# A gated-recurrence and expert kernel on one core: a new written-out order, first exponentials by halves of the heads, and two more turns by DMA

## The chip, the cores and the metric

One core of one Trainium2 chip. The metric is device microseconds of one execution. The kernel before has run three times: 178.1, 178.4 and 218.8 us, median 178.4. A further execution was profiled; it took 177.89 us, of which the profile covers a span of 176.1 us.

## The reference

Two stages follow each other. A gated linear recurrence over 768 steps, for 4 batches of 8 heads of width 48, and then a two-layer expert with a SiLU between:

```python
f = 1.0 / (1.0 + np.exp(-f_logit))
for t in range(S):                      # S = 768
    state = f[:, :, t, :, None] * state + np.einsum('bhd,bhe->bhde', k[:, :, t], v[:, :, t])
    y[:, :, t] = np.einsum('bhd,bhde->bhe', q[:, :, t], state)
...
x = y.transpose(0, 2, 1, 3).reshape(3072, 384)
h = x @ w_in                            # 384 x 2048
out = (h * sigmoid(h)) @ w_out          # 2048 x 384
```

## The kernel before, in words

**Tiling.** The 768 steps are cut into 6 chunks of 128, so there are 24 *units* (chunk, batch). Two units make a *pair* P, units 2P and 2P+1. In the first three pairs (units 0 to 5) the two units are two neighbouring chunks of one batch, loaded as one *block* whose rows on a partition are two steps; from unit 6 on they are the same chunk of two batches.

**One unit** is a chain of small tasks. Their names are used all through this text; `_u` is the unit, `_P` the pair.

- `f`, `k`, `q`, `v`: loads, issued on SP (L257). `E`, `L`: exponential and logarithm of the gate on ACT (L264, L266 for blocks, L268 for the rest); they give the logarithms `lf`.
- `csh_P` (a block, L335 to L339) and `cs_u` (L372, L376): running sums of `lf` over the chunk, a product with a triangle on PE. `ia`, `a` and `al` (L379, L381, L384) are exponentials of these sums, with either sign, on ACT.
- `ki`, `qg` (L386, L390): k and q times these factors, on DVE or POOL, into a buffer `qk`. Both have then to be turned (heads' width to the partitions). This is done on PE, `tq` (8 transposes, L395), with copies `qc`, `kc` or `qkc` out of PSUM (L396 to L405), or by a DMA transpose from SP, `qkD` (L407). Units 0 to 7 go by PE, units 8 to 23 by DMA.
- `sc2_P` (L280): the scores of both units of a pair, 16 matmuls. `at` (L416): their mask, two per unit, on DVE. `vb`: v in bf16.
- `y_u` (L422 with the state from before, L426): the unit's output. `d_u` (L448; in blocks from a copy of k that `dT` and `kn` turn back), `sd`, `su` (L453 to L461): the next state.
- y has to be turned as well: copied out of PSUM by `yc`, then turned on PE by `yT` (3 transposes, L434) and copied by `xc`, or by a DMA transpose, `yD` (L442). Units 0 to 13 and 22, 23 go by PE, 14 to 21 by DMA.
- `mi` (L323, 256 columns, both units of a pair at once) and `mi1` (L313, one unit, 128 columns, in the first three pairs): x times w_in, in 8 groups of a pair or 4 of a unit. `si`, `si1` (L320, L310): SiLU on ACT. `mo` (L351): times w_out, four quarters of 4 matmuls; `moh` (L357) the same by halves for the last pair. `oc`, `och`: copies out of PSUM; `so`, `soh`: stores.
- `wi`, `wo`: loads of the weights in pieces; `wic`, `woc`: their casts to bf16, in three parts each, spread over ACT, DVE and POOL. The four groups `mi1_u_0` to `mi1_u_3` need pieces 0 and 1, piece 2, piece 3 and piece 4 of w_in.
- `idle_i_n_w`: n matmuls with zeros of w columns (L291), which fill PE's waits in the first 15 us. They compute nothing.

**The order** is written out by hand: the string `PLAN` (L32 to L104) lists every task as `name/engine/slots`, and each engine runs its own tasks in that order; the slots say which numbered buffer (of 8 PSUM banks, 5 `qk` buffers, and so on, L28) a task takes. An engine does not run ahead of a task that waits. ACT needs another function table for SiLU than for exponentials and logarithms, and a table load stands wherever the order goes from one to the other (L467 to L473, issued at L499).

## Time and profile before

| what | value |
|---|---|
| profiled execution, and its span | 177.89 us, 176.1 us |
| PE (matmuls) busy | 169.5 us, 96% |
| PEld (weight loads) busy | 133.6 us, 76% |
| ACT busy | 133.3 us, 76% |
| DVE busy | 97.7 us, 55% |
| POOL busy | 59.1 us, 34% |
| ACT table loads after the first | 17, 21.8 us together |
| DMA transposes | 16 of q and k, 8 of y |
| first matmul, first one that is not fill | 1.19 us, 5.98 us |

Busy time of PE is that of overlapping matmuls: one of 384 columns is shown with 326 ns, yet twelve in a row take 1.95 us. So the step from one matmul to the next, as the chain of waits gives it for runs of equal ones, says what PE's work costs. Times in the text are microseconds from the start of the span.

### The profile page before, as it was taken

To read this page: it belongs to the slowest core of one execution; us is meant where nothing else is said; L and a number is where in the kernel's file an instruction comes from. 1 tells how busy PE (TensorE), PEld (TensorE's weight loads), DVE (VectorE), ACT (ScalarE), POOL (GpSimd) and SP (SyncE) were. 2 spreads that over 40 slices of the span, in tenths; PEclk is the share of its full clock that TensorE was granted. 3 is DMA by queue.
4 is the path that set the end of the run, shared out by engine and by line. 5 is a ranking of instruction groups with operands and counts; after the bars stand their busy time and mean duration, and the time that the engine had idled before them with its cause. 6 is when DMAs were issued, how large, how long until landed. Compare 5 with 4: busy or idle time off the path is not lost.

```text
span 176.1 us, 4798 instructions
## 1 busy us (share of the span) xinstructions
PE 169.5 (96%) x1952; PEld 133.6 (76%) x1952; DVE 97.7 (55%) x201; ACT 133.3 (76%) x249; POOL 59.1 (34%) x91
## 2 busy tenths in 40 slices
...
GB/s 147 325 286 259 397 387 220 397 207 169 217 199 241 182 238 221 159 233 232 152 197 165 251 227 89 273 176 210 137 153 99 206 162 138 217 147 0 92 90 89
DMA packets 115541, 35.17 MB, mean 200 GB/s; under 512 B 110752, under 2 KB 113056, under 8 KB 115520
## 3 DMA queue, kind: packets, MB, share of 16 engines
...
q8 instruction: 15, 0.25, 0.5%
...
HBM read 25.17 MB, written 4.72 MB: 170 GB/s over the span
## 4 chain that ended last, share of the span: by engine, by line
PE 73%; SPq 8%; DMA 8%; DVE 5%; issue 2%; POOL 2%; ACT 0%; POOLq 0%; DVEq 0%
PE ps L351 27%; PE ps L323 22%; PE ps L313 8%; SPq L257 6%; DMA wh<-in_moe_w_in_dram 5%; PE ps L280 3%; PE ps L357 3%; DMA qkT<-qk 3%; PE ps L426 2%; SPq L442 2%; DVE st L242 2%; PE ps L422 2%; PE ps L372 1%; DVE at L416 1%; PE ps L448 1%
## 5 line engine op out<-in xcount | busy, mean ns | idle before, releaser
L351 PE MATMUL ps<-w_out,hT 128*128 128x384 bf16 x352 | 66.4, 326 | 0.0
L323 PE MATMUL ps<-xT,w_in 128*128 128x256 bf16 x432 | 52.4, 273 | 0.0
L323 PEld LDWEIGHTS <-w_in 128*128 128x128 bf16 x432 | 45.3, 110 | 3.9 <-DMA xT<-yb 0.3
L320 ACT ACTIVATE hT<-ps 128x512 bf16<-128x512 f32 x72 | 39.0, 603 | 10.3 <-PE ps L323 9.6
L351 PEld LDWEIGHTS <-hT 128*128 128x128 bf16 x352 | 31.7, 97 | 16.6 <-ACT hT L310 0.3
L416 DVE TENSOR_TENSOR at<-ps,triu 128x512 bf16<-128x512 f32 x36 | 22.5, 683 | 19.8 <-PE ps L280 18.8
L242 POOL TENSOR_TENSOR qk<-q,av 128x384 bf16<-128x384 f32 x15 | 15.4, 1033 | 42.2 <-DMA q<-in_q_dram 25.0
L499 ACT ACT_TABLE_LOAD x17 | 21.8, 1283 | 0.3
L313 PE MATMUL ps<-xT,w_in 128*128 128x128 bf16 x288 | 17.9, 219 | 0.9 <-POOL w_in L239 0.6
L313 PEld LDWEIGHTS <-w_in 128*128 128x128 bf16 x288 | 16.6, 110 | 1.3 <-POOL w_in L239 0.8
L242 POOL TENSOR_TENSOR qk<-k,ia 128x384 bf16<-128x384 f32 x12 | 12.7, 1066 | 13.4 <-DMA k<-in_k_dram 8.7
L381 ACT ACTIVATE av<-ps 128x384 f32<-128x384 f32 x24 | 11.9, 504 | 3.5 <-PE ps L376 1.8
L237 DVE CAST yb<-ps 128x384 bf16<-128x384 f32 x16 | 8.8, 555 | 10.2 <-PE ps L426 9.0
L264 ACT ACTIVATE f<-f 128x768 f32<-128x768 f32 (+1 forms) x13 | 10.3, 796 | 5.4 <-DMA f<-in_f_logit_dram 5.3
L310 ACT ACTIVATE hT<-ps 128x512 bf16<-128x512 f32 x24 | 13.2, 607 | 1.6 <-PE ps L313 1.5
L453 DVE TENSOR_TENSOR sd<-ps,st 128x384 f32<-128x384 f32 x16 | 8.8, 553 | 9.5 <-ACT hT L320 4.7
L369 POOL DMA_DIRECT2D out_dram<-ob x14 | 8.0, 573 | 17.9 <-DVE ob L237 14.3
L242 POOL TENSOR_TENSOR st<-sd,al 48x192 bf16<-48x192 f32 x18 | 9.8, 543 | 8.7 <-PE ps L422 5.1
L379 ACT ACTIVATE ia<-ps 128x384 f32<-128x384 f32 x24 | 11.8, 505 | 0.0
L237 DVE COPY ob<-ps 128x384 f32<-128x384 f32 x14 | 7.7, 553 | 7.4 <-PE ps L351 3.6
L239 POOL CAST vb<-v 128x384 bf16<-128x384 f32 x11 | 5.6, 507 | 14.6 <-DMA v<-in_v_dram 13.2
L242 DVE TENSOR_TENSOR qk<-k,ia 128x384 bf16<-128x384 f32 x12 | 7.1, 605 | 5.1 <-ACT ia L379 4.2
...
## 6 DMA issues: line engine op xcount, KB each, us to landing
...
```

The source lines that it names most:

```text
L237: nc.vector.tensor_copy(o, i)
L242: (nc.vector if eng == "DVE" else nc.gpsimd).tensor_mul(*a)
L257: nc.sync.dma_start(out=dst, in_=src)
L310: return nc.scalar.activation(at("hT", u // 2)[:, 4 * m:4 * m + 4, i * C:(i + 1) * C], h, AF.Silu)
L313: nc.tensor.matmul(h[:, n, :], w_in_tile(4 * m + n, kk), at("xT", u // 2)[:, kk, i * C:(i + 1) * C], start=(kk == 0), stop=(kk == KT - 1))
L320: return nc.scalar.activation(at("hT", P)[:, 2 * j:2 * j + 2, :], h, AF.Silu)
L323: nc.tensor.matmul(h[:, i, :], w_in_tile(2 * j + i, kk), at("xT", P)[:, kk, :], start=(kk == 0), stop=(kk == KT - 1))
L351: nc.tensor.matmul(o, at("hT", P)[:, n, i * C:(i + 1) * C], w_out_sb[n // 4][:, n % 4, :], start=(n == 0), stop=(n == NT - 1))
L379: nc.scalar.activation(at("ia", u).rearrange("p h d -> p (h d)"), at("cs", u)[:, 0:HD], AF.Exp)
L381: nc.scalar.activation(at("av", u).rearrange("p h d -> p (h d)"), at("cs", u)[:, 0:HD], AF.Exp, scale=-1.0)
L416: nc.vector.tensor_mul(at("at", u)[:, r], at(f"s{r}", u).rearrange("p (n c) -> p n c", c=C), (triup if two else triu)[:, None, :].to_broad ...
L499: nc.scalar.preload_act_table_set(turn[n])
```

## The change

1. **Units turned by DMA.** q and k of unit 7 (`tq_7`, `qkc_7` become `qkD_7`) and y of unit 13 (`yT_13`, `xc_13` become `yD_13`).
2. **Halves of the heads.** In the three blocks each exponential and each logarithm is two instructions of four heads (`Eh`, `Lh`) instead of one of eight; 12 ACT instructions instead of 6. Loads stay whole.
3. **A new order.** Every line of `PLAN` differs: the order within each engine, the slots, and for many tasks the engine. Of `yc` 14 are on ACT (8 before), of `qg` 15 on DVE (9 before), 19 table loads follow the first on ACT (17 before). The fill is 29 matmuls of 512 columns and 6 of 256 (22 and 4 before). The first weights are now pieces 3 and 4 of w_in, then 1, 0 and 2, then w_out; before they were 2, 1, 0 of w_in, two pieces of w_out, and then 4 and 3.
4. `HALF = 3` becomes the set `BLOCKS = {0, 1, 2}` with the same meaning. Other new branches (weights by POOL, scores of one unit, loads of half the heads) are used by no task of the new order.

```diff
-HALF = 3
+BLOCKS = {0, 1, 2}
...
 PLAN = """
-f_0_1/SP/0 f_2_3/SP/1 k_0_1/SP/0 q_0_1/SP/0 E_0_1/ACT L_0_1/ACT/0 E_2_3/ACT idle_0_11_512/PE/0 csh_0/PE/0,1 f_4_5/SP/2 q_2_3/SP/1 v_0/SP/0 k_2_3/SP/1
...
+f_0_1/SP/0 f_2_3/SP/1 k_0_1/SP/0 q_0_1/SP/0 Eh_0_0/ACT Eh_0_1/ACT v_2/SP/0 Lh_0_0/ACT/0 Lh_0_1/ACT Eh_2_0/ACT idle_0_11_512/PE/0 csh_0/PE/0,1
...
+    def half_logs(kind, u, hf):
+        P, hs = u // 2, slice(4 * hf, 4 * hf + 4)
+        if kind == "Eh":
+            e = at("f", P).rearrange("p a h d -> p (a h d)").rearrange("p (h w) -> p h w", h=H)[:, hs]
+            nc.scalar.activation(e, e, AF.Exp, scale=-1.0)
+        else:
+            nc.scalar.activation(at("lf", P)[:, :, hs, 0:D], pairs("f", P)[:, :, hs], AF.Ln, bias=1.0)
...
+        if kind in ("Eh", "Lh"):
+            return half_logs(kind, *a)
...
-    TABLE = {**dict.fromkeys(("E", "L", "ia", "a", "al"), "natural_log_exp_and_others"), "si": "silu_and_others", "si1": "silu_and_others"}
+    TABLE = {**dict.fromkeys(("E", "L", "Eh", "Lh", "ia", "a", "al"), "natural_log_exp_and_others"), "si": "silu_and_others", "si1": "silu_and_others"}
```

The order at the start. These are DVE's rows of the kernel before, from the copies of turned q and k of the first block to the copy `xT` that the first `mi1` needs (at_115 and at_116 are the masked scores of units 0 and 1, sd a state's increment, ps a PSUM bank, yb and xT the unit's output before and after it is turned):

```order
L237 COPY qkT_112<-ps_68 128x512
L237 COPY qkT_112<-ps_67 128x8x64
L416 TENSOR_TENSOR at_115<-ps_64,triup 128x512
L416 TENSOR_TENSOR at_115<-ps_66,triup 128x512
L455 COPY sd_122<-ps_63 128x384
L416 TENSOR_TENSOR at_116<-ps_61,triup 128x512
L416 TENSOR_TENSOR at_116<-ps_68,triup 128x512
L237 COPY qkT_113<-ps_62 128x8x64
L237 COPY qkT_113<-ps_61 128x512
L237 COPY qkT_113<-ps_63 128x8x64
L237 CAST yb_120<-ps_68 128x384
L237 COPY xT_139<-ps_62 128x3x2x64
```

And DVE's rows of the change, up to its first `xT`, that of unit 1 (at_116 is unit 0 here, at_117 unit 2; st is a state, kn the keys turned back):

```order
L436 TENSOR_TENSOR at_116<-ps_66,triup 128x512
L238 COPY qkT_113<-ps_63 128x8x64
L475 COPY sd_122<-ps_68 128x384
L436 TENSOR_TENSOR at_116<-ps_65,triup 128x512
L436 TENSOR_TENSOR at_117<-ps_62,triup 128x512
L436 TENSOR_TENSOR at_117<-ps_67,triup 128x512
L243 TENSOR_TENSOR st_146<-sd_122,al_124 48x4x48 x2
L473 TENSOR_TENSOR sd_123<-ps_66,st_146 128x384
L238 COPY kn_133<-ps_62 128x512
L238 CAST yb_120<-ps_65 128x384
L243 TENSOR_TENSOR st_146<-sd_123,al_124 48x4x48 x2
L238 COPY xT_139<-ps_65 128x3x2x64
```

The masks of unit 2 and the state update of unit 0 now stand ahead of the output `yb` of unit 1, and the update of unit 1 ahead of `xT`. Before, the masks of unit 2 came behind both, the update of unit 0 was on POOL, and that of unit 1 came later.

ACT's first rows, before (f_69, f_70 are the gates of the first two blocks, lf_92 and lf_93 their logarithms; ia and av are the factors made from the running sums):

```order
L264 ACTIVATE f_69<-f_69 128x768
L266 ACTIVATE lf_92<-f_69 128x16x48
L264 ACTIVATE f_70<-f_70 128x768
L266 ACTIVATE lf_93<-f_70 128x16x48
L379 ACTIVATE ia_95<-ps_61 128x384
L379 ACTIVATE ia_96<-ps_62 128x384
L381 ACTIVATE av_98<-ps_61 128x384
```

and in the change:

```order
L276 ACTIVATE f_69<-f_69 128x384 x2
L278 ACTIVATE lf_92<-f_69 128x2x4x48 x2
L276 ACTIVATE f_70<-f_70 128x384
L278 ACTIVATE lf_93<-f_70 128x2x4x48
L276 ACTIVATE f_70<-f_70 128x384
L401 ACTIVATE av_98<-ps_62 128x384
L399 ACTIVATE ia_95<-ps_62 128x384
L401 ACTIVATE av_99<-ps_61 128x384
L278 ACTIVATE lf_93<-f_70 128x2x4x48
L404 ACTIVATE al_124<-ps_61 128x8
L399 ACTIVATE ia_96<-ps_61 128x384
```

The last half of the second block's logarithms, which `csh_1` needs, now stands behind three factors of the first block.

Later, ACT's rows around the factors of units 14 and 15, before (the rows from the logarithms of pair 8 to the next table load; ia_97 and ia_96 are of units 14 and 16; the factors of unit 15 stand a long way ahead of them):

```order
L264 ACTIVATE f_72<-f_72 128x768
L268 ACTIVATE lf_94<-f_72 128x16x48
L235 COPY xT_140<-ps_63 128x3x128
L235 COPY ob_135<-ps_62 128x384
L379 ACTIVATE ia_97<-ps_66 128x384
L381 ACTIVATE av_98<-ps_65 128x384
L384 ACTIVATE al_127<-ps_65 128x4
L381 ACTIVATE av_99<-ps_66 128x384
L379 ACTIVATE ia_96<-ps_65 128x384
L499 ACT_TABLE_LOAD
```

and in the change (av_99 and ia_97 first are unit 15, ia_96 and av_99 in the last rows unit 14, av_100 unit 17):

```order
L401 ACTIVATE av_99<-ps_65 128x384
L399 ACTIVATE ia_97<-ps_65 128x384
L404 ACTIVATE al_127<-ps_68 128x4
L404 ACTIVATE al_128<-ps_67 128x4
L399 ACTIVATE ia_96<-ps_68 128x384
L404 ACTIVATE al_124<-ps_65 128x4
L404 ACTIVATE al_129<-ps_63 128x4
L401 ACTIVATE av_100<-ps_67 128x384
L401 ACTIVATE av_99<-ps_68 128x384
L519 ACT_TABLE_LOAD
```

Between `cs_14`, from which the factors of unit 14 are made, and `sc2_7`, which needs its turned q and k, PE has in the change only `d_13`, `yT_12`, two quarters `mo` and seven groups `mi`; before, it had 36 tasks there.

More of the change, by code (lines that the diff above doesn't have):

```diff
@@ L32 @@
 PLAN = """
-f_0_1/SP/0 f_2_3/SP/1 k_0_1/SP/0 q_0_1/SP/0 E_0_1/ACT L_0_1/ACT/0 E_2_3/ACT idle_0_11_512/PE/0 csh_0/PE/0,1 f_4_5/SP/2 q_2_3/SP/1 v_0/SP/0 k_2_3/SP/1
-v_2/SP/1 v_1/SP L_2_3/ACT/1 ia_0/ACT/0 ia_1/ACT/1 a_0/ACT/0 idle_1_3_512/PE/2 csh_1/PE/2,3 al_2/ACT/0 a_1/ACT/1 a_2/ACT/2 ki_0/DVE/0 ki_1/DVE/1
-qg_2/POOL/2 qg_0/DVE qg_1/DVE idle_2_4_512/PE/4 tq_0/PE/4,5 tq_1/PE/6,7 kc_0/DVE/0 ia_3/ACT/2 E_4_5/ACT a_3/ACT/0 al_0/ACT/1 qc_0/ACT kc_1/DVE
-qc_1/DVE L_4_5/ACT/2 ia_2/ACT/0 vb_0/POOL/0 wi_2/SP/0 idle_3_4_512/PE/1 dT_0/PE/1 sc2_0/PE/5,3,0,7 csh_2/PE/4,6 qg_3/POOL/3 ki_3/POOL ki_2/POOL
@@ L37 @@
-kn_0/ACT/0 d_0/PE/2 wi_1/SP/0 wi_0/SP/1 at_0_1/DVE/0 at_0_0/DVE sd_0/DVE/0 at_1_0/DVE/1 su_0/POOL/0 idle_4_2_256/PE/1 y_0/PE/3 tq_3/PE/1,5
-idle_5_2_256/PE/2 tq_2/PE/2,0 wo_0/SP/1 a_4/ACT/1 ia_5/ACT/1 al_4/ACT/2 kc_3/ACT/1 at_1_1/DVE qc_3/DVE vb_1/ACT/1 a_5/ACT/2 yc_0/ACT/0 ia_4/ACT/2
-kc_2/DVE qc_2/DVE y_1/PE/7 dT_2/PE/5 yT_0/PE/1 sc2_1/PE/6,0,3,2 wo_1/SP/2 wic_2_2/POOL wic_2_0/POOL yc_1/DVE/1 wic_2_1/ACT vb_2/ACT/2 xc_0/DVE/0
-at_2_0/DVE/2 at_2_1/DVE dT_1/PE/4 yT_1/PE/7 dT_3/PE/1 mi1_0_1/PE/6 wi_4/SP/3 y_2/PE/0 xc_1/ACT wic_1_0/ACT wic_0_0/ACT kn_1/DVE/1 kn_2/DVE/0
```

161 lines of the change are left out of this document (89 added, 72 removed).

## The prediction

> **What bounds the kernel now.** I read the page's first part, then the stretches of time, then the chain of waits and the timelines of PE, ACT and DVE for the first 22 us.
>
> ```profile
> span 176.1 us, 4798 instructions
> PE 169.5 (96%) x1952; PEld 133.6 (76%) x1952; DVE 97.7 (55%) x201; ACT 133.3 (76%) x249; POOL 59.1 (34%) x91
> ```
>
> ```profile
> 20.00:50.00 30.00, 29.47 (x420) 24.03 (x418) 20.43 (x42) 24.78 (x49) 12.10 (x17) 1.00 1.00 276
> 50.00:170.00 120.00, 119.88 (x1311) 96.34 (x1309) 63.73 (x118) 92.11 (x167) 38.67 (x55) 1.00 0.87 176
> ```
>
> The columns of the second fence are the stretch, its length, then PE, PEld, DVE, ACT and POOL busy, the granted clock, the DMA share. From 50 to 170 us PE idles 0.12 us and its clock is full: no other order can gain there. PE is the bound; the others wait for it.
>
> What PE's work costs is read from equal runs in the chain of waits (start, length, line, count):
>
> ```profile
> 28.31 2.68 PE ps L313 x48
> 148.33 3.93 PE ps L323 x36
> 152.26 1.95 PE ps L351 x12
> 35.14 0.45 PE ps L395 x8
> 154.21 0.55 PE ps L280 x16
> 158.30 0.20 PE ps L426 x8
> 158.13 0.17 PE ps L422 x4
> ```
>
> So a group `mi1` (12 matmuls) takes 0.67, a group `mi` (6) 0.655, a quarter `mo` (4) 0.65, `tq` (8 transposes) 0.45, `dT` and `yT` with 4 and 3 of them 0.23 and 0.17, `sc2` 0.55, `y` 0.20, or 0.37 with a state, and `d`, four matmuls of the form of L422, 0.17. With them I ask of any start on PE how much work lay ahead of it; the rest of the time is lost, to waits and fill. The start shows it:
>
> ```profile
> 1.19 4.57 PE L291 MATMUL ps<-zero 128*128 128x512 bf16 x11 [1.19 <-DVE zero L477]
> 5.98 0.32 PE L335 MATMUL ps<-lf,tri 128*128 128x384 bf16 x1 [0.22 <-ACT lf L266]
> 6.83 0.81 PE L291 MATMUL ps<-zero 128*128 128x512 bf16 x3
> 7.58 0.32 PE L335 MATMUL ps<-lf,tri 128*128 128x384 bf16 x1
> 11.89 0.62 PE L280 MATMUL ps<-qkT 48*128 48x128 bf16 x16
> 18.96 0.86 PE L313 MATMUL ps<-xT,w_in 128*128 128x128 bf16 x12 [0.59 <-POOL w_in L239]
> 21.34 0.84 PE L313 MATMUL ps<-xT,w_in 128*128 128x128 bf16 x12 [0.30 <-ACT w_in L235]
> ```
>
> `csh` takes 0.85 (5.98 to 6.83). At 21.34 us PE has done three `csh` (2.55), four `tq` (1.8), four `dT` (0.9), two `sc2` (1.1), `d_0` and `d_2` (0.34), `y_0`, `y_1`, `y_2` (0.77), three `yT` (0.5), two `mi1` (1.34): 9.3. So 12.0 us are lost by then, which is nearly all that the span holds beside work and end: idle after 20 us is 0.53 and 0.12. Only the start can hold more than 1% of the time.
>
> **The change part by part.**
>
> *Turns by DMA.* `tq_7` (0.45) and `yT_13` (0.17) leave PE: −0.6, on the engine that bounds. DVE or ACT loses two copies, off the path. In their place come a transpose of q, k and one of y:
>
> ```profile
> qkT<-qk SPq DMA_TRANSPOSE x16, 4.4
> xT<-yb SPq DMA_TRANSPOSE x8, 2.3
> L407 SPq DMA_TRANSPOSE qkT<-qk x16: 1231/1269/3565, 57.0 to 148.7; - x16
> DMA to landing us min/median/max: 3.2/4.4/5.7
> ```
>
> (The last two rows belong to the tile qkT.) Each blocks SP's queue for 1.27 us at the median, and lands 4.4 or 2.3 after its issue. `qkD_7` has from the factors of unit 7 to `sc2_3` 8.7 us of PE work, `yD_13` from `y_13` to `mi_6_3` 5.5: both fit, so nothing is added on the path. Cover gone, each costs at most its latency, 4.4 and 2.3.
>
> *Halves of the heads.* A half is of the form that the loads of single units already have:
>
> ```profile
> L264 ACT ACTIVATE f<-f 128x384 f32<-128x384 f32 x2 | 1.1, 525 | 0.0
> ```
>
> and ACT's first rows in time:
>
> ```profile
> 4.21 0.84 ACT L264 ACTIVATE f<-f 128x768 f32<-128x768 f32 x1 [2.19 <-DMA f<-in_f_logit_dram]
> 5.08 0.84 ACT L266 ACTIVATE lf<-f 128x768 bf16<-128x768 f32 x1
> 5.83 0.83 ACT L264 ACTIVATE f<-f 128x768 f32<-128x768 f32 x1
> 7.44 0.85 ACT L379 ACTIVATE ia<-ps 128x384 f32<-128x384 f32 x2
> 8.18 0.49 ACT L381 ACTIVATE av<-ps 128x384 f32<-128x384 f32 x1
> 14.61 0.73 ACT L235 COPY qkT<-ps 128x512 bf16<-128x512 bf16 x1 [0.18 <-PE ps L395]
> 15.20 0.51 ACT L235 CAST vb<-v 128x384 bf16<-128x384 f32 x1
> ```
>
> A whole exponential and the logarithm that waits for it start 0.87 apart. Of halves, four start about 0.44 apart (an estimate: 525 ns less the overlap of about 0.09 that the whole ones show, 0.84 long and 0.75 apart) and need not wait for each other; the last ends near 6.05 against 5.92. So the halves alone cost 0.1 us on the first sum. Off the path the rest is hidden by PE's fill.
>
> *The order of the start.* The gate of the first block lands as before. I walk ACT from 6.05: three halves of block 1 (to 7.5), then `a_1`, `ia_1`, `a_0` at 0.37 each (7.44 to 8.18 is two), and only then the fourth half, to 9.05. So `csh_1` starts at 9.1; before, it started at 7.58. `a_2` follows at 10.05, `ia_3`, `ia_2` (its buffer comes free with `ki_1`, the fourth product on DVE since 8.7, two of which take 1.03: 11.1), `a_3`, then copies at 0.59 (14.61 to 15.20), an exponential between them: `qc_1` ends at 14.0, and `sc2_0`, which needs it, starts there and not at 11.89. Then DVE, with steps from these rows:
>
> ```profile
> 7.95 1.03 DVE L242 TENSOR_TENSOR qk<-k,ia 128x384 bf16<-128x384 f32 x2 [3.92 <-ACT ia L379]
> 13.75 0.56 DVE L455 COPY sd<-ps 128x384 f32<-128x384 f32 x1
> 14.22 1.28 DVE L416 TENSOR_TENSOR at<-ps,triup 128x512 bf16<-128x512 f32 x2
> 15.42 1.36 DVE L237 COPY qkT<-ps 128x512 bf16<-128x512 bf16 x3
> 18.82 0.74 DVE L237 COPY kn<-ps 128x512 bf16<-128x512 bf16 x2
> 17.16 0.57 DVE L237 COPY xT<-ps 128x384 bf16<-128x384 bf16 x1
> L242 DVE TENSOR_TENSOR st<-sd,al 48x192 bf16<-48x192 f32 x22 | 9.7, 440 | 0.3
> ```
>
> A mask costs 0.60 (two from 14.22 to 15.42), `sd` 0.47 (13.75 to 14.22) and `yc`, which moves as much, the same, `kn` or `qc` 0.34, `xc` 0.57, and a state update 0.75 (two of 0.44, overlapped a little like the rest). From 14.7 DVE has, in the change's order without a pause, six masks (3.6), `qc_2` (0.34), `sd_0`, `sd_1`, `yc_1` (1.4), `kn_3` (0.34), `su_0`, `su_1` (1.5) and `xc_1` (0.6): 7.8, to 22.5. `y_1` waits there for `su_0` (19.6), `yT_1` for `yc_1` (21.0), the first `mi1` stands behind `yT_1`, and the second, `mi1_1_3`, needs `xc_1`: it starts at 22.55. Ahead of it lies what lay ahead of 21.34, with `d_1` for `d_2` and one `mi1` less: 8.6. Lost: 13.9, against 12.0. That is **+1.9 us**.
>
> The weights bound this from below:
>
> ```profile
> 17.64 0.62 ACT L235 CAST w_in<-ws 128x512 bf16<-128x512 f32 x1 [0.78 <-DMA ws<-in_moe_w_in_dram]
> ```
>
> The first piece stands, as now, behind ten loads of the same size, so it lands at 17.6; three casts and a `yc` on ACT end at 20.2. Were DVE's chain no hindrance, the first `mi1` could start then, with 7.9 ahead: 12.3 lost, +0.3. From above: fourteen DVE steps with a tenth of a us of waiting each, an estimate from the 0.10 to 0.25 that lie between steps handed over in the rows, +3.3. I take the walk, since each of its steps has a row.
>
> *From there to 47 us.* Before, `mi1_4_0` starts at 47.00:
>
> ```profile
> 47.00 0.22 PE L313 MATMUL ps<-xT,w_in 128*128 128x128 bf16 x1
> ```
>
> Between 21.34 and 47.00 lie 14 `mi1` (9.4), 16 `mo` (10.4) and 5.0 of small tasks: 24.8 of 25.7, so 0.9 are lost. In the change the late weights have had two us more when PE asks, and all sums stand far ahead of their use: I take **−0.7**; bounds −0.9, and +0.3 if a cast comes late.
>
> *After 47 us.* PE's idle was 0.12; it can only grow. In the change the way from a unit's sum to its scores is short: behind `cs_14` PE has `yT_12`, `d_13`, two `mo` and seven `mi`, 6.2 us, until `sc2_7`; behind `cs_22` one `mo`, eight `mi`, one `mo`, 6.5, until `sc2_11`; behind `cs_11` 9.2. In these ACT makes `ia` and `a` (`a_14` is the ninth in its row, done 2.3 after `cs_14`), DVE the product (0.8, of which 0.5 by the row at 7.95 and the rest handovers), then SP issues, and the transpose lands 3.2 to 5.7 later: 6.3 to 8.8 against 6.2 for `sc2_7`, so 0.1 to 2.6; for `sc2_11` 5.4 to 7.9 against 6.5. I take **+0.4**, near the short end, as two transposes in a row share what precedes them; the bound is +4.
>
> *Table loads.* Two more at 1.3 us on ACT:
>
> ```profile
> L499 ACT ACT_TABLE_LOAD x17 | 21.8, 1283 | 0.3
> ```
>
> 2.6 us of an engine that is 24% idle; PE's banks cover them. If that cover were gone they would cost 2.6.
>
> *The end* is the same four halves and copies; 0, within 0.3.
>
> The sum: +1.9 −0.7 −0.6 +0.4 = **+1.0 us**, so 178.9 for the profiled execution's 177.9. The median of the runs, 178.4, is 0.5 above that; beside it the sum gives **179.4 us**.
>
> **The rivals.**
>
> *The start waits for weights alone (22%).* DVE's chain is not in the way, and the loss is +0.3, with nothing late after: +0.3 −0.7 −0.6 = −1.0, 177.4. For it: the first `mi1` waited for a cast before (the row at 18.96). Against: DVE's 7.8 us without a pause.
>
> *Turned q and k come late (14%), and the kernel is slower.* The transposes take 5.7 us as the longest did, and stand behind loads on SP. Then `sc2_7` waits 2.6, `sc2_11` 1.4, and `sc2_5` (9.2 us, two pairs' four transposes in a row at 1.27 each) 0.6: 4.6 in place of 0.4, 183.6. It decides from a landing of about 5 us on. For it: the maximum in the row of qkT; against: the median, 4.4.
>
> *The clock drops at the start (4%).* Between 14 and 22 us PE has less work than time. The two rows of stretches above grant the full clock, 1.00, but eleven fill matmuls take 4.57 at first, 0.42 each, and three from 6.83 on take 0.81, 0.27 each: PE starts at half rate and gets full. If it fell back for some 4 us of work, that would cost 2.0: 181.4. Against: no wait in the walk is over 1 us. The Trainium skill ("TensorE: Matmul & The Clock Gate", section "What's actually happening") says that an idle window of about 3.4 us puts PE back to half rate; by that rule waits of under 1 us leave the clock full and the sum as it stands. No run here shows such a drop.
>
> *The new order starts so well that it gains over 2% (3%).* It would have to take 3.6 of the 12.0 lost: 174.8. Against: the weights' landing at 17.6.
>
> **How the numbers follow.** My forecast holds 57%. A measurement tells about 2%, 3.6 us, from no change. The likeliest time is 179.4. The range takes in the first rival's 177.4 with 0.4 for the end and the casts, and on the upper side most of the way to the late turns: 177.0 to 183.0. Faster by over 2% is the last rival and a little of the first: 0.04. Slower by over 2%, over 182.0, is three quarters of the late turns and the upper end of forecast and clock: 0.14. The same: 0.82.
>
> **What would show it.** In the changed profile `csh_1` should start near 9.1, `sc2_0` near 14.0, the second `mi1` near 22.5, and DVE be busy from 14.7 to 22.5 with hardly a pause. A dense stretch that starts before 21 us proves the walk wrong. A wait of PE for the DMA of qkT over 1 us at the scores of pairs 5, 7 or 11 proves the late turns. ACT should have 20 table loads, none ahead of a wait of PE; idle of PE after 50 us under 1 us.

## The result, and the profile after

The change takes 183.9 us at the median of four runs (182.9 to 185.4), the kernel before 178.2 beside it. The ratio is 1.032, with a 95% interval of 1.027 to 1.037: slower by 3.2%, outside the range of the prediction. Here and below a ratio leaves disturbed executions out, while a median counts them all, so the two can differ a little. The profiled execution took 182.9 us, its span 181.1, against 177.9 and 176.1 before. The first lines of the page after:

```profile
span 181.1 us, 4805 instructions
PE 170.5 (94%) x1948; PEld 134.1 (74%) x1950; DVE 93.0 (51%) x192; ACT 140.8 (78%) x268; POOL 53.8 (30%) x87
```

PE is busy one us longer in a span that is five longer, so it mostly waits more. The stretches of the kernel after, with the columns of those in the prediction:

```profile
20.00:50.00 30.00, 28.94 (x410) 23.82 (x411) 20.17 (x41) 27.70 (x54) 9.10 (x15) 1.00 0.98 269
50.00:170.00 120.00, 116.90 (x1285) 92.75 (x1283) 59.29 (x110) 94.19 (x176) 39.84 (x58) 1.00 0.90 180
```

PE idles 3.1 us between 50 and 170, where it idled 0.12. The timeline of PE after (start, length, line, tiles, count, and in brackets the wait ahead with what ended it) shows where:

```profile
9.03 0.32 PE L355 MATMUL ps<-lf,tri 128*128 128x384 bf16 x1 [0.19 <-ACT lf L278]
14.13 0.62 PE L290 MATMUL ps<-qkT 48*128 48x128 bf16 x16
21.69 0.83 PE L331 MATMUL ps<-xT,w_in 128*128 128x128 bf16 x12
23.36 0.33 PE L454 MATMUL ps<-ident,yb 128*128 128x128 bf16 x3 [0.83 <-DVE xT L238]
23.52 2.67 PE L331 MATMUL ps<-xT,w_in 128*128 128x128 bf16 x45
100.87 0.34 PE L454 MATMUL ps<-ident,yb 128*128 128x128 bf16 x3 [0.23 <-DVE yb L238]
103.01 4.78 PE L341 MATMUL ps<-xT,w_in 128*128 128x256 bf16 x42 [0.49 <-DVE xT L238]
114.13 0.40 PE L290 MATMUL ps<-qkT 48*128 48x128 bf16 x8 [0.52 <-DMA qkT<-qk]
161.23 0.62 PE L290 MATMUL ps<-qkT 48*128 48x128 bf16 x16 [1.86 <-DMA qkT<-qk]
```

These are `csh_1`, `sc2_0`, the first `mi1`, `yT_2`, the second `mi1`, then `yT_12`, the first `mi` of pair 6, the second half of `sc2_8`, and `sc2_11`. Below, "lost" at a step is what it was in the prediction: its start less the PE work that lies ahead of it in the order.

| lost, us | before | after | difference |
|---|---|---|---|
| when the dense stretch begins (21.3, 23.4 us) | 12.0 | 14.85 | +2.85 |
| from there to 47 us | 0.9 | 0.25 | −0.65 |
| from 47 us to PE's last step | 1.2 | 4.75 | +3.55 |
| PE's work | 158.8 | 158.15 | −0.6 |
| end | 3.3 | 3.15 | −0.15 |

The sum is +5.0, the difference of the spans. Of the 4.75 after 47 us, 3.75 lie at four places: 0.4 at `yT_12`, 0.65 at the `mi` of pair 6, 0.7 at `sc2_8`, 2.0 at `sc2_11` (the brackets show the larger part of each; some of the rest shows in no bracket).

What stood ahead of these places, in the timeline of DVE and POOL after:

```profile
21.34 1.34 DVE L243 TENSOR_TENSOR st<-sd,al 48x192 bf16<-48x192 f32 x2
22.71 0.59 DVE L238 COPY xT<-ps 128x384 bf16<-128x384 bf16 x1
98.05 2.18 DVE L243 TENSOR_TENSOR st<-sd,al 48x192 bf16<-48x192 f32 x4
152.83 1.40 DVE L243 TENSOR_TENSOR st<-sd,al 48x192 bf16<-48x192 f32 x2
20.72 1.18 POOL L240 CAST w_in<-ws 128x512 bf16<-128x512 f32 x2 [5.14 <-DMA ws<-in_moe_w_in_dram]
21.84 1.66 POOL L240 CAST w_in<-wh 128x384 bf16<-128x384 f32 x3
99.01 1.00 POOL L243 TENSOR_TENSOR qk<-k,ia 128x384 bf16<-128x384 f32 x1 [9.09 <-issue]
152.66 1.00 POOL L243 TENSOR_TENSOR qk<-k,ia 128x384 bf16<-128x384 f32 x1 [8.63 <-ACT ia L399]
```

Updates of a state (`su_1`; `su_12` and `su_11`; `su_18`) stand ahead of `xc_1`, `yc_12` and `qg_22`, which PE or a turn waits for. `su_12` takes 0.72 us, which is two halves of about 355 ns, the median of all halves; `su_1`, `su_11` and `su_18`, which run beside the work of POOL in the lower rows, take 1.34, 1.43 and 1.40.

The DMA engines' load moved to later. The same stretches of the kernel before:

```profile
100.00:115.00 15.00, 15.00 (x150) 12.35 (x149) 8.47 (x17) 14.14 (x25) 5.81 (x8) 1.00 0.91 205
115.00:140.00 25.00, 24.88 (x278) 20.24 (x276) 14.67 (x27) 18.84 (x32) 4.80 (x8) 1.00 0.83 158
140.00:160.00 20.00, 20.00 (x194) 14.94 (x193) 7.80 (x13) 11.51 (x22) 4.19 (x5) 1.00 0.69 158
```

and of the kernel after:

```profile
100.00:115.00 15.00, 13.76 (x154) 10.33 (x152) 8.67 (x17) 10.79 (x23) 7.04 (x11) 1.00 1.00 172
115.00:140.00 25.00, 25.00 (x257) 19.98 (x256) 12.22 (x23) 18.50 (x34) 6.77 (x11) 1.00 0.92 170
140.00:160.00 20.00, 19.38 (x185) 15.58 (x183) 7.51 (x13) 16.79 (x31) 6.99 (x12) 1.00 0.91 210
```

The last two columns are the DMA share and GB/s. From 140 to 160 us it is 0.91 where it was 0.69: stores and the last loads crowd where the last turns must land. These are readings of two traces; the runs below test them.

### The profile page after: what moved, and what is told of

It is laid out like the page before. It is cut to its first block, busy times and chain, and to the rows that moved or that the text cites. A ratio compares the mean times of both kernels' runs of the same rounds, so it can differ in the third digit from the quotient of the medians.

```text
span 181.1 us, 4805 instructions
## 1 busy us (share of the span) xinstructions
PE 170.5 (94%) x1948; PEld 134.1 (74%) x1950; DVE 93.0 (51%) x192; ACT 140.8 (78%) x268; POOL 53.8 (30%) x87
## 4 chain that ended last, share of the span: by engine, by line
PE 74%; DMA 11%; DVE 8%; SPq 4%; issue 2%; POOL 0%; ACT 0%; DVEq 0%
PE ps L371 28%; PE ps L341 21%; PE ps L331 9%; DMA qkT<-qk 6%; SPq L259 4%; PE ps L290 3%; PE ps L377 3%; DMA q<-in_q_dram 3%; DVE st L243 2%; PE ps L446 2%; PE ps L442 2%; DMA v<-in_v_dram 2%; DVE at L436 2%; PE ps L468 2%; PE ps L392 1%
## 5 line engine op out<-in xcount | busy, mean ns | idle before, releaser
L371 PE MATMUL ps<-w_out,hT 128*128 128x384 bf16 x352 | 64.8, 326 | 0.0
L341 PE MATMUL ps<-xT,w_in 128*128 128x256 bf16 x432 | 50.0, 273 | 0.5 <-DVE xT L238 0.5
L338 ACT ACTIVATE hT<-ps 128x512 bf16<-128x512 f32 x72 | 37.9, 615 | 7.8 <-PE ps L341 7.4
L436 DVE TENSOR_TENSOR at<-ps,triu 128x512 bf16<-128x512 f32 x36 | 22.5, 684 | 25.9 <-PE ps L290 17.0
L243 POOL TENSOR_TENSOR qk<-k,ia 128x384 bf16<-128x384 f32 x14 | 14.0, 1006 | 45.0 <-ACT ia L399 30.5
L243 POOL TENSOR_TENSOR qk<-q,av 128x384 bf16<-128x384 f32 x9 | 9.5, 1064 | 19.8 <-DMA q<-in_q_dram 14.8
L238 DVE COPY ob<-ps 128x384 f32<-128x384 f32 (+1 forms) x14 | 7.2, 523 | 14.7 <-PE ps L377 9.2
L243 DVE TENSOR_TENSOR qk<-q,av 128x384 bf16<-128x384 f32 x15 | 8.4, 571 | 12.1 <-ACT av L401 8.2
L236 ACT CAST yb<-ps 128x384 bf16<-128x384 f32 x14 | 6.6, 476 | 9.7 <-issue 5.1
L389 POOL DMA_DIRECT2D out_dram<-ob x14 | 8.0, 575 | 18.9 <-ACT ob L236 16.7
L328 ACT ACTIVATE hT<-ps 128x512 bf16<-128x512 f32 x24 | 12.6, 615 | 0.7 <-PE ps L331 0.6
L243 POOL TENSOR_TENSOR st<-sd,al 48x192 bf16<-48x192 f32 x20 | 10.5, 523 | 2.9 <-DVE sd L475 1.2
L303 PE MATMUL ps<-zero 128*128 128x512 bf16 (+1 forms) x33 | 9.1, 415 | 1.3 <-DVE zero L497 1.2
```

The lines of the kernel that those rows point to most:

```text
L243: (nc.vector if eng == "DVE" else nc.gpsimd).tensor_mul(*a)
L303: nc.tensor.matmul(at("idle", u)[:, 0:w], zero[:, 0:128], zero[:, 0:w], start=True, stop=True)
L328: return nc.scalar.activation(at("hT", u // 2)[:, 4 * m:4 * m + 4, i * C:(i + 1) * C], h, AF.Silu)
L338: return nc.scalar.activation(at("hT", P)[:, 2 * j:2 * j + 2, :], h, AF.Silu)
L341: nc.tensor.matmul(h[:, i, :], w_in_tile(2 * j + i, kk), at("xT", P)[:, kk, :], start=(kk == 0), stop=(kk == KT - 1))
L371: nc.tensor.matmul(o, at("hT", P)[:, n, i * C:(i + 1) * C], w_out_sb[n // 4][:, n % 4, :], start=(n == 0), stop=(n == NT - 1))
```

## The experiments

Each row of an edit names one engine's tasks in their order. The medians of the kernel before lay between 177.9 and 178.8. A line of three dots marks a cut in an edit. "Lost at the end" is read from the one profiled execution of a run, as in the table above; it is 14.1 for the kernel before and 19.8 for the change.

| run | us | ratio to before, 95% | lost at the end |
|---|---|---|---|
| halves_alone | 178.0 | 0.998 to 1.002 | 14.2 |
| start_before | 182.6 | 1.014 to 1.029 | 19.0 |
| turns_undone | 183.8 | 1.027 to 1.037 | 19.4 |
| su_late | 180.7 | 1.011 to 1.020 | 18.4 |
| pool_off | 183.7 | 1.019 to 1.037 | 20.4 |
| stores_early | 183.7 | 1.026 to 1.036 | 20.5 |
| chains_early | 190.4 | 1.059 to 1.074 | 27.7 |
| mended | 189.3 | 1.058 to 1.069 | 25.4 |
| mended3 | 186.3 | 1.034 to 1.047 | 23.1 |
| y0_first | 180.9 | 1.012 to 1.020 | 18.5 |
| best | 186.5 | 1.039 to 1.050 | 23.7 |
| turns_alone | 181.1 | 1.008 to 1.018 | 19.9 |
| turn7_clear | 179.5 | 1.005 to 1.012 | 15.5 |
| turns_clear | 182.7 | 1.022 to 1.030 | 19.5 |
| stores_clear | 182.0 | 1.018 to 1.027 | 18.9 |
| joined | 181.7 | 1.014 to 1.024 | 19.4 |
| mended4 | 180.3 | 1.007 to 1.015 | 17.2 |
| joined2 | 180.6 | 1.008 to 1.018 | 18.4 |

### The halves alone, on the kernel before

```diff
 ACT
-E_0_1 L_0_1 E_2_3 L_2_3
+Eh_0_0 Eh_0_1 Lh_0_0 Lh_0_1 Eh_2_0 Eh_2_1 Lh_2_0 Lh_2_1
...
```

> The kernel before, with only its three exponentials and three logarithms of blocks cut into halves of the heads, in the same places of the same order. Theory A (the halves cost nothing that counts; the start is lost to the order around them): 178.2 plus 0 to 0.4, the first csh at about 6.1 and the second near 7.8. Rival B (six more instructions on ACT ahead of every later step at the start are what moves the second csh from 7.6 to 9.0): 179.4 to 180.5.

178.0, ratio 1.000, the second `csh` at 7.56. Theory A holds: the halves cost nothing. `csh_1` is at 9.03 in the change because ACT has `a_1`, `ia_1` and `a_0` between the last exponential and the last logarithm that it needs.

### The start of before in the changed kernel

The first line of `PLAN`, all engines together:

```diff
-f_0_1 f_2_3 k_0_1 q_0_1 Eh_0_0 Eh_0_1 v_2 Lh_0_0 Lh_0_1 Eh_2_0
+f_0_1 f_2_3 k_0_1 q_0_1 E_0_1 L_0_1 E_2_3
...
```

> The changed kernel with the order of the kernel before up to PE's 39 us (whole exponentials and logarithms, the loads and PE's first steps as before), and the change's order from there on. Theory A (the start's order costs 2.85 us of the 5.0, and what comes later is lost there by itself): 2.0 to 2.9 us under the changed kernel's 183.9, so 181.0 to 181.9, with the lost time at 46 us near 12.9 and again some 3 to 4 us lost between 95 us and the end. Rival B (PE's lead at the start is only lent: what is won there is waited away later for the same transfers and loads): within 0.8 us of 183.9.

182.6: 1.3 under the change, between the two. At 41 us 13.0 are lost where the change has 14.9, at the end 19.0 against 19.8. Of the lead of 1.9 more than half was waited away: 0.5 at `y_4`, near the seam of the two orders, 0.6 at `y_10`, whose v had not landed. Then `sc2_11` waits about as long as in the change:

```profile
160.41 0.62 PE L290 MATMUL ps<-qkT 48*128 48x128 bf16 x16 [2.02 <-DMA qkT<-qk]
```

Neither theory holds by itself: the start costs about 2 us where it is lost, and a lead does not all arrive.

### The turns undone in the changed kernel

```diff
-qkD_7/SP yD_13/SP
+tq_7/PE qkc_7/DVE yT_13/PE xc_13/DVE
```

> The changed kernel, with q, k of unit 7 and y of unit 13 turned on PE again (8 and 3 transposes, two copies on DVE), all else in the change's order. Theory A (both turns land in time and save PE 0.6 us): 183.9 plus 0.5 to 0.7, so 184.5. Rival B (the two turns hold SP's queue for 1.3 us each and make later loads and turns late): 183.9 minus 0.3 to 1.5, with shorter waits at the scores of pairs 8 and 11.

183.8, no difference, with an interval of 0.9 us to either side; the 0.6 of PE is back, and the waits have moved (0.8 ahead of `cs_14` for the bank that the new copy holds, 1.2 at `sc2_7` instead of 0.5 at `sc2_8`). This run tells nothing apart; the turns were tried again, in the order of before.

### The updates of the state behind

```diff
 DVE
-yc_1 su_1 xc_1
+yc_1 xc_1 su_1
...
-sd_12 su_12 su_11 yc_12 qg_15 ki_15 xc_12 qg_14 sd_13 oc_10
+sd_12 yc_12 qg_15 ki_15 xc_12 qg_14 su_11 sd_13 oc_10 su_12
...
-sd_18 su_18 qg_22 ki_22
+sd_18 qg_22 ki_22 su_18
```

> The changed kernel, with four updates of the state on DVE (su of units 1, 11, 12 and 18) put behind the copies and products that PE or a turn waits for: behind xc_1, behind qg_14, behind oc_10 and behind ki_22. Theory A (these updates stand ahead of what PE waits for, and take 1.3 to 1.5 us instead of 0.71 because POOL works in the same memory at that time): yT_2's wait of 0.83, yT_12's of 0.39 and mi_6_3's of 0.66 go, and the turn of unit 22 is issued 0.7 earlier, so 1.2 to 2.5 us under 183.9: 181.4 to 182.7. Rival B (the waits have other causes, weights at the start and the transfers at the end): within 0.6 us of 183.9.

180.7: 3.1 under the change, more than theory A gave. Its four runs lie within 1 us (180.5 to 181.5), the change's within 2.5. The waits at `yT_2`, `yT_12` and pair 6 are gone, and what its profiled execution still waits for is

```profile
75.97 0.36 PE L446 MATMUL ps<-vb,at 128*128 128x48 bf16 x8 [0.92 <-ACT vb L236]
114.14 0.40 PE L290 MATMUL ps<-qkT 48*128 48x128 bf16 x8 [1.64 <-DMA qkT<-qk]
159.83 0.62 PE L290 MATMUL ps<-qkT 48*128 48x128 bf16 x16 [0.44 <-DMA qkT<-qk]
```

The scores of pair 8 stand at 114.14, as they did at 114.13: the lead of 1.1 us that PE had there was waited away for the turn. What stayed came from the turn of unit 22, 0.3 earlier and 1.1 shorter. The two profiled executions differ by 1.4 only, so 1.7 of the 3.1 lie in executions that no trace shows. Nor is all of the lead at the start the edit's: 0.47 us of it is there before `sc2_1`, ahead of the first moved update, in an execution whose first loads landed up to 0.5 earlier.

### POOL's work taken from beside the updates

```diff
-wic_1_1/POOL wic_1_0/POOL ki_17/POOL ki_14/POOL
+wic_1_0/ACT wic_1_1/ACT ki_14/DVE ki_17/DVE
```

> The changed kernel with the state's updates where the change has them, but without POOL's work beside three of them: the casts wic_1_1 and wic_1_0 on ACT behind kn_2, and ki_14 and ki_17 on DVE behind xc_12 and sd_13. Theory A (an update takes 0.71 us with POOL idle and 1.3 to 1.5 with POOL at work, and that is the lateness): su_1 under 1.1 us, su_12 and su_11 0.71 to 0.75 each, xc_1 and yc_12 earlier by 0.4 to 0.8, the waits at yT_2, yT_12 and mi_6_3 (1.9 in all) down to 0.8 or less. Rival B (the updates are as long whatever POOL does; they read and write 48 lanes at a time): su_11 still 1.4, the waits as before.

The timeline of its DVE:

```profile
21.36 0.71 DVE L243 TENSOR_TENSOR st<-sd,al 48x192 bf16<-48x192 f32 x2
98.38 1.47 DVE L243 TENSOR_TENSOR st<-sd,al 48x192 bf16<-48x192 f32 x4
```

The same instructions at the same place take 0.71 to 0.74 each; `su_18`, which still has `ki_23` beside it, takes 1.41. So the length is POOL's doing, and theory A is shown; `yT_2`'s loss falls from 1.0 to 0.4 and those of pair 6 go. But the time is 183.7. The 0.6 won at `yT_2` was lost again at 27.79 us, where PE waited for a SiLU that ACT did no earlier than in the change (0.56). What was won at pair 6 went at two later places:

```profile
114.31 0.40 PE L290 MATMUL ps<-qkT 48*128 48x128 bf16 x8 [1.46 <-DMA qkT<-qk]
161.86 0.62 PE L290 MATMUL ps<-qkT 48*128 48x128 bf16 x16 [2.30 <-DMA qkT<-qk]
```

### The stores around the last turn

```diff
 SP
-yD_20 yD_21 so_5 so_14 qkD_23 qkD_22 so_13 so_18
+yD_20 yD_21 qkD_23 qkD_22 so_13 so_18
 POOL
-so_8 su_17 ki_23 so_19 so_16 so_17
+so_8 so_14 so_16 su_17 ki_23 so_19 so_17
```

> The changed kernel with three stores taken away from the time around the last turn: so_5 right behind so_4 on SP, so_14 and so_16 right behind so_8 on POOL. Theory A (the turn of unit 22 takes 5.84 us to land because the stores' packets are in its way): it lands within 4 us, and the wait at sc2_11 falls from 2.02 to 0.5 or less: 182.3 to 182.9. Rival B (it is late because it is issued late): it still lands after 5 us or more, and the time stays within 0.5 us of 183.9.

183.7; the turn lands 5.34 after its issue, still slow, and `sc2_11` loses 1.0. Not decided, as `so_19`, `so_17` and `so_13` were still there. So a later run took these away as well:

```diff
 SP
-yD_21 qkD_23 qkD_22 so_13 so_18 so_21
+yD_21 qkD_23 qkD_22 so_21 so_13 so_18
 POOL
-ki_23 so_19 so_17 so_15
+ki_23 so_15 so_19 so_17
```

> The changed kernel with no store issued between 145 and 158 us: so_5, so_14 and so_16 early (behind so_4 and so_8), so_13 and so_18 on SP behind so_21, so_19 and so_17 on POOL behind so_15. Theory A (the stores' packets hold the turn of unit 22 back): it lands within 4 us of its issue instead of 5.84, and the wait at sc2_11 is under 0.6: 182.2 to 183.0. Rival B (its own issue, at 155.35, is what is late, and any second turn of a pair takes so long there): over 5 us and a wait over 1.2 still.

182.0, 1.9 under the change. The line of the turns, for the turn of unit 22 alone in the change:

```profile
L427 SPq DMA_TRANSPOSE qkT<-qk x1: 1418/1418/1418, 155.4 to 155.4; - x1
DMA to landing us min/median/max: 5.8/5.8/5.8
```

and for the turns of units 23 and 22 here:

```profile
L427 SPq DMA_TRANSPOSE qkT<-qk x2: 1232/1232/1232, 154.1 to 155.8; - x2
DMA to landing us min/median/max: 3.0/3.1/3.2
```

Unit 22's, the later one, takes 3.2 instead of 5.8, with the issue 0.45 later than in the change. `sc2_11` does not wait. Theory A is shown: the stores held the last turn back; by what way they did, no run tells.

### Loads ahead of turns: three attempts that lost

```diff
 SP
-qkD_8 qkD_9 qkD_11 qkD_10 f_12_13 v_10_11
+v_10_11 qkD_8 qkD_9 qkD_11 qkD_10 f_12_13
...
-v_20_21 qkD_21 qkD_20 f_22_23 k_22_23 q_22_23
+v_20_21 f_22_23 k_22_23 q_22_23 qkD_21 qkD_20
 POOL
-ki_17 ki_14 qg_16 su_13 ki_16 qg_17
+ki_17 qg_16 ki_14 ki_16 qg_17 su_13
...
```

> The changed kernel with loads and steps of late turns put earlier, the state's updates where the change has them: v_10_11 ahead of qkD_8, q_16_17 right behind k_16_17, f, k and q of units 22 and 23 ahead of qkD_21, POOL's qg_16, ki_16 and qg_17 ahead of su_13, cs_23 and cs_22 right behind mo_18_1, a_22 ahead of vb_22. Theory A (the turns of pairs 8 and 11 are late because their loads stand behind waiting turns on SP and their steps behind others): the wait of 0.69 at sc2_8 and of 2.02 at sc2_11 go, 1.5 to 2.7 us under 183.9: 181.2 to 182.4. Rival B (DVE's slowed updates of the state alone make them late): within 0.6 us of 183.9, sc2_11 still waits over 1.5.

190.4, the opposite. Three loads ahead of `qkD_21` made it late by itself:

```profile
L427 SPq DMA_TRANSPOSE qkT<-qk x1: 4257/4257/4257, 144.4 to 144.4; - x1
DMA to landing us min/median/max: 6.2/6.2/6.2
```

SP had spent 5 us on the three loads, the turn's issue took 4.26 instead of 1.27, it landed 1.2 us behind the last load, and PE waited:

```profile
151.91 1.03 PE L290 MATMUL ps<-qkT 48*128 48x128 bf16 x16 [5.41 <-DMA qkT<-qk]
```

The theory that the loads of the last pair stood too late on SP falls: behind the turns, where the change has them, they do less harm. For pair 8 this run decides nothing: `sc2_8` did not wait, but PE came to it 0.9 later than in the change. Of the 27.7 lost, 2.1 are a halved clock behind the long wait (last section). Joined with the late updates and the early stores:

> The changed kernel with the updates of the state behind, the loads and steps of the late turns ahead, and the three stores early, all at once; its start is the change's. Theory A (each of the waits has its own cause, and their sum, 0.8 at yT_2, 1.05 at yT_12 and mi_6_3, 0.69 at sc2_8, 2.0 at sc2_11, comes back): 183.9 less 3.8 to 4.6, so 179.3 to 180.1; the order at the start remains, some 1.5 us over the kernel before. Rival B (a lead that PE wins is waited away at the next transfer): not under 180.7, which the updates alone gave.

189.3: `sc2_10` waited 4.9, and the clock halved again behind it. Then with k and q of the last pair left behind `qkD_20`, and `v_10_11` only ahead of `f_12_13`:

> The changed kernel with the updates of the state behind, and of the earlier loads only those that SP can issue without a turn queuing behind them: v_10_11 right behind qkD_10, q_16_17 right behind k_16_17, f of units 22 and 23 alone ahead of qkD_21 (their k and q stay behind qkD_20); POOL's qg_16, ki_16 and qg_17 ahead of su_13, cs_23 and cs_22 right behind mo_18_1, a_22 ahead of vb_22. Theory A (the 5 us that the earlier run of this kind lost came from k and q of the last pair standing ahead of qkD_21 on SP): sc2_10 waits under 0.3, sc2_8 under 0.5, sc2_11 under 0.5, y_10 under 0.4; 178.8 to 180.0. Rival B (every lead is waited away): 180.4 to 181.2, as with the updates alone.

186.3. Now `f_12_13` landed at 75.8 instead of 73.0, and ACT, which takes its tasks in the order of PLAN, held the copy of y behind the exponential of f:

```profile
75.81 0.84 ACT L266 ACTIVATE f<-f 128x768 f32<-128x768 f32 x1 [5.37 <-DMA f<-in_f_logit_dram]
76.56 0.46 ACT L236 CAST yb<-ps 128x384 bf16<-128x384 f32 x1
```

PE waited 2.3 us for that y at 77.1, and 1.8 at `sc2_10`, where f still stood ahead of the turn. Behind the wait of 2.3 the clock fell to half (last section).

### The first y ahead, at the start

```diff
 DVE
-kn_0 at_1_1 at_1_0 at_0_0 qc_2 sd_0 at_0_1
+kn_0 at_0_0 at_0_1 qc_2 at_1_1 at_1_0 sd_0
 PE
-d_0 idle_5_6_512 sc2_1 d_1 csh_2 y_0 dT_3 y_2 y_1 yT_0
+d_0 y_0 idle_5_3_512 sc2_1 d_1 yT_0 csh_2 dT_3 y_2 y_1
```

> The changed kernel with the four updates of the state behind as in the run that moved them alone, and in the first 18 us the chain of unit 0 ahead: DVE takes at_0_0, at_0_1 and qc_2 before at_1_1 and at_1_0, PE y_0 right behind d_0 and yT_0 right behind d_1, ACT yc_0 before Lh_4_0 and xc_0 before wic_3_2, three of the six idle matmuls of 512 ahead of sc2_1 left out. Theory A (the change's start is late since PE's and DVE's order makes the first y wait until 18.9 us, behind csh_2): the first mi1 starts at 20.5 or earlier instead of 21.7, the lost time at mi1_1_3 falls by 0.4 to 1.2, and so does the end, 179.5 to 180.4. Rival B (the weights' landing sets the start): mi1_1_3 no earlier than with the updates alone, about 22.4, and the time as there, 180.7.

180.9, as with the updates alone; the first `mi1` at 22.24, later than with those (21.22). In the profiled execution q of the second block landed at 13.2, 0.8 later than there, and `tq_3` waited 1.0 for the product made of it. So the time is rival B's, but not its cause: the first `mi1` started right behind `yT_1` without a wait, so no weight held it. How much the order did and how much that load, the trace does not tell. Joined with mended3:

> The two runs before it joined: the updates of the state behind, the loads that can go earlier, and the chain of unit 0 ahead at the start. Theory A (the losses add up): 183.9 less 3.1 for the updates, 0.7 to 1.9 for the late turns and 0.4 to 1.2 for the start: 177.7 to 179.7, within 1% of the kernel before, whose order still loses less at the start. Rival B (a lead at the start is waited away): within 0.4 of the run without the start's edit.

186.5, as without it.

### The turns by DMA, on the kernel before

```diff
 DVE
-qkc_6 oc_3 sd_5 oc_2 qg_7 ki_7
+qg_7 ki_7 qkc_6 oc_3 sd_5 oc_2
...
 SP
-f_12_13 v_7 v_8_9
+f_12_13 qkD_7 v_7 v_8_9
...
-f_18_19 f_20_21 so_7
+f_18_19 f_20_21 yD_13 so_7
```

> The kernel before, with only q, k of unit 7 and y of unit 13 turned by DMA: qg_7 and ki_7 ahead of qkc_6 and the turn right behind them on SP, yc_13 ahead of sd_13 and the turn of y ahead of so_7; all else in the order of before. Theory A (the turns save PE its 0.62 us of transposes where they land in time): 178.1 less 0.3 to 0.6, 177.5 to 177.8, no wait over 0.3 at sc2_3 or at the first mi of pair 6. Rival B (a turn on SP's queue makes the loads and turns behind it late by more than PE saves): 178.5 to 180, with a wait over 0.7 us for a DMA at sc2_3, at pair 6 or at sc2_8.

1.3% slower, 0.8 to 1.8. Theory A falls. The profiled execution is the slowest of the six (183.0 us), so its waits may be longer than those behind the 1.3%:

```profile
57.98 0.40 PE L280 MATMUL ps<-qkT 48*128 48x128 bf16 x8 [2.47 <-DMA qkT<-qk]
105.74 2.14 PE L323 MATMUL ps<-xT,w_in 128*128 128x256 bf16 x18 [1.14 <-DMA xT<-yb]
```

and the turn of unit 7 in it:

```profile
L407 SPq DMA_TRANSPOSE qkT<-qk x1: 3599/3599/3599, 51.2 to 51.2; - x1
DMA to landing us min/median/max: 6.7/6.7/6.7
```

Its product was ready at 50.1; SP was still issuing `f_12_13`, then the turn's issue took 3.6, and it landed 2.3 us behind that load. Is it the loads ahead? With unit 7 alone turned by DMA, and `k_8_9`, `f_12_13` and `v_7` behind it:

```diff
 SP
-q_8_9 k_8_9 f_12_13 qkD_7 v_7 v_8_9
+q_8_9 qkD_7 k_8_9 f_12_13 v_7 v_8_9
```

> The kernel before with only q, k of unit 7 turned by DMA: qg_7 and ki_7 ahead of qkc_6, the turn right behind them, and on SP the loads k_8_9, f_12_13 and v_7 behind the turn instead of ahead of it. Theory A (the turn lands some 2 us behind the load that is ahead of it; with f_12_13 and k_8_9 behind, only q_8_9 is ahead): it lands within 4.2 us of its issue, by 54.5, sc2_3 waits under 0.4, and the time is 178.0 less 0.1 to 0.5, so 177.5 to 177.9. Rival B (a turn is slow among loads of either side): it lands after 5 us or more and sc2_3 waits over 1: 178.8 to 180.5.

```profile
L407 SPq DMA_TRANSPOSE qkT<-qk x1: 1791/1791/1791, 49.5 to 49.5; - x1
DMA to landing us min/median/max: 3.2/3.2/3.2
```

It lands in 3.2, and `sc2_3` does not wait: for the turn itself theory A is shown. The kernel is 0.8% slower all the same. In part this is `v_7`, which, now behind, came late:

```profile
59.05 0.33 PE L448 MATMUL ps<-vb,qk 128*128 128x96 bf16 x4 [0.48 <-POOL vb L239]
```

A further 1.1 us went around the scores of pair 4, whose turn of unit 8 was issued 1.9 later; the trace names only 0.28 of that, and in halves_alone 0.5 went there though no turn had been added. With y of unit 13 as well, `f_18_19`, `f_20_21` and `so_7` behind its turn:

> The same, with y of unit 13 turned by DMA as well, f_18_19, f_20_21 and so_7 behind its turn on SP. Theory A: the turn of y lands within 2.6 us of its issue and the first mi of pair 6 waits under 0.4: 177.3 to 177.9. Rival B (loads put behind turns are late themselves, f_18_19 and f_20_21 above all): a wait over 0.5 us at the mi of pair 6 or at the scores of pairs 8 and 9: 178.4 to 180.

2.6% slower: 1.2 at the `mi` of pair 6, which waited for the turn of y though that took only 3.3, and another 1.9 inside it. The 1.9 is rival B's: `f_18_19`, now behind the turn, landed at 105.7 instead of 99.7, and ACT held the SiLUs of pair 6 behind its exponential:

```profile
105.71 0.84 ACT L264 ACTIVATE f<-f 128x768 f32<-128x768 f32 x1 [6.57 <-DMA f<-in_f_logit_dram]
```

In this order the two turns, which replace 0.62 us of PE's work, cost more than that at both of the places tried.

### Do the losses add up?

The start of before, the late updates and no store near the last turn:

> The order of before up to PE's 39 us, then the change's, with the four updates of the state behind and with no store around the last turn. Theory A (the losses add up: 1.3 for the start as the run of that alone gave, 3.1 for the updates, 0.5 to 1.4 for the last turn): 183.9 less 4.6 to 5.8, 178.1 to 179.3, as the kernel before within 1%. Rival B (what one wins is waited away at the next turn or load): 179.8 or more.

181.7: no, the time is rival B's. PE waits 1.7 for the turn of unit 17, until 113.66 where the change had 114.13, and later 1.1 for the logarithm of the last pair, whose f landed at 149.9. The last two runs free the turn of unit 17 and bring that f ahead:

```diff
 SP
-q_14_15 f_18_19 yD_13 q_16_17 qkD_15 qkD_14 v_16_17 qkD_16 qkD_17
+q_14_15 q_16_17 f_18_19 yD_13 qkD_15 qkD_14 qkD_16 qkD_17 v_16_17
...
-k_20_21 yD_19 yD_18 v_20_21 qkD_21 qkD_20 f_22_23
+k_20_21 f_22_23 yD_19 yD_18 v_20_21 qkD_21 qkD_20
 POOL
-ki_17 ki_14 qg_16 su_13 ki_16 qg_17
+ki_17 ki_14 qg_16 ki_16 qg_17 su_13
```

> The changed kernel with the four updates of the state behind, no store around the last turn, q_16_17 ahead of f_18_19 on SP, POOL's qg_16, ki_16 and qg_17 ahead of su_13 (none of them earlier than ki_14), their turns right behind, ahead of v_16_17, and f of units 22 and 23 ahead of yD_19, where SP has nothing to issue. Theory A (the turn of unit 17 holds PE at 114.1 whatever its lead, and the last turn falls away too): 180.7 with the updates alone, less 1.0 to 1.9 at sc2_8 and 0.6 at sc2_11: 178.4 to 179.4. Rival B (another transfer, late for the same full DMA engines, takes its place): 180.0 or more, with a new wait over 1 us.

180.3, the best of the changed kernels; the time is rival B's, but no single new wait reaches 1 us. `qkD_17` lands at 109.9 instead of 114.1, neither `sc2_8` nor `sc2_11` waits, and two turns of y, behind the loads that went ahead, wait instead:

```profile
101.85 4.75 PE L341 MATMUL ps<-xT,w_in 128*128 128x256 bf16 x42 [0.48 <-DMA xT<-yb]
139.00 4.12 PE L341 MATMUL ps<-xT,w_in 128*128 128x256 bf16 x36 [0.65 <-DMA xT<-yb]
```

> The same with the order of before up to PE's 39 us. Theory A (with no turn late, the start's lead of 1.2 to 1.9 us reaches the end): 1 to 1.6 under mended4, 177.2 to 178.4, no slower than the kernel before. Rival B: within 0.5 of mended4, or over it.

180.6, the same as mended4, although it has lost 1.1 less at 41 us:

```profile
76.04 0.36 PE L445 MATMUL ps<-vb,at 128*128 128x48 bf16 x8 [1.10 <-ACT vb L235]
103.01 4.75 PE L340 MATMUL ps<-xT,w_in 128*128 128x256 bf16 x42 [0.85 <-DMA xT<-yb]
117.94 10.02 PE L340 MATMUL ps<-xT,w_in 128*128 128x256 bf16 x90 [0.80 <-DMA xT<-yb]
```

A load of v and two turns take the lead back. None of the eighteen beats the kernel before.

## Why the prediction was wrong, point by point

**What bounds the kernel.** "No other order can gain there" fits PE's 0.12 us of idle and is half of the matter: between 50 and 170 us an order could only lose, and this one lost. The DMA share of 1.00 and 0.87 stood in the quoted stretches and went unused; the runs show that a transfer's landing there depends on its neighbours (the last turn took 5.8 us with stores beside it, 3.2 without).

**Turns by DMA, −0.6.** In the change itself both turns were in time: unit 7's landed at 55.5 for scores at 56.9, that of y 13 at 100.7 for an `mi` at 103.0, and PE's work is 0.6 less. But "both fit, so nothing is added on the path" was argued from their own latency. In the order of before they fit by the same reckoning, and cost 1.3%; and undoing them in the change left its time as it was (183.8), so that the 0.6 reached the end is not shown.

**Halves, +0.1.** Measured 0.0, within 0.4.

**The start, +1.9.** Measured +2.85. `csh_1` (9.1 forecast, 9.03) and `sc2_0` (14.0, 14.13) came out; the latter for another reason, as `tq_3`, ahead of it on PE, waited for q of the second block, which SP loads behind v and f. The second `mi1`, forecast at 22.5, started at 23.5: `su_1` in the walk cost 0.75 and took 1.34 beside POOL's casts. With `su_1` moved behind, `yT_2` started at 22.07 instead of 23.36, of which 0.47 was won ahead of it. So the walk was right in its steps, and the term short by that one and by the handovers (its upper bound was +3.3). The rival of the clock did not come: the change's granted clock is 1.00 in all stretches. The rival of weights alone is out: the last cast for the first `mi1` ended at 20.7, and PE reached that step at 21.69, behind `yT_1`.

**25 to 47 us, −0.7.** Measured −0.65.

**After 47 us, +0.4: the step that failed.** Measured +3.55. The term took late turns alone, priced near their median landing, at pairs 5, 7 and 11. The bound of +4 that stood beside it would have held this, but the range, up to 183.0, took in less. Pairs 5 and 7 were in time. Pair 11 lost 2.0, pair 8, which was not on the list, 0.7, and both turns landed 5.6 to 5.9 after their issue. For pair 11 the cause is shown: stores beside the turn (5.8 us, 3.2 without them), and `su_18` ahead of its product, slowed by POOL. For pair 8 freeing the products of unit 17 from the update ahead of them on POOL, its q from the turn of y ahead of it on SP, and its turns from the load between, took the wait away; which of the three did most was not tried apart. The 1.05 at `yT_12` and pair 6 came from updates beside POOL's work, a cause that was nowhere in the prediction.

**Table loads and end, 0.** There are 20 loads, as forecast, and no wait of PE behind one; the end is 0.15 shorter.

The rival of late turns (14%) gave 183.6, near the measured 183.9, but with 2.6 us at `sc2_7`, where nothing was late, and none for the updates: its price came out, its places mostly did not, so that the total is near is in good part luck. Its sign did come at one place, a wait over 1 us for qkT at pair 11 (1.86), and idle of PE after 50 us, which was to stay under 1, was 3.1. What the sum of terms missed is that they are not independent: where a run took one loss away (su_late, pool_off, joined2), PE gave much of the lead back at the next turn or load. The second half of `sc2_8` began at 114.13, 114.14, 114.15, 114.31 and 114.29 in the change, su_late, y0_first, pool_off and stores_clear, though PE came to these scores between 112.1 and 113.2. It is no fixed time, however: it was 115.0 in stores_early and 113.7 in joined, and in start_before, with the change's order there, the turn of unit 17 landed at 112.1 and `sc2_8` did not wait.

**What stays open.** mended4 still loses 3.2 us more than before, 1.6 of it by 41 us, and joined2 shows that taking the start away only moves the wait. Which order of loads would carry such a lead to the end was not found. How much of su_late's 3.1 us is the last turn is not settled either, since its profiled execution shows 1.4.
